# Gated attention and channel MLP on one core: q and k stored by SyncE, ten shared x/y tiles, and another order of the attention

## The chip, the cores and the metric

The kernel runs on one core of a Trainium2 chip. A core has five engines that run side by side and meet at semaphores: TensorE (PE in the profile) multiplies matrices into the accumulator memory PSUM, VectorE (DVE), ScalarE (ACT) and GpSimd (POOL) work elementwise, and SyncE (SP) issues transfers; ScalarE issues some too. The metric is the device time of one execution in microseconds, as the median of several runs.

## The reference, cut to what matters

The input x has 2048 tokens of 512 features. Two branches are computed from it and mixed per token.

```python
qkv = (x @ wqkv)                        # 32 heads of 16 features
scores = q k^T / 4, masked to 0 <= i - j < 256
a = softmax(scores) v, heads joined, @ wo
y = layernorm(x)                        # no scale, no shift
b = gelu(y @ w1 + b1) @ w2 + b2         # 512 -> 1792 -> 512
g = sigmoid(sum(x * gate_w))
out = g * a + (1 - g) * b
```

## The kernel before

Every matmul of the projections and of the MLP is made of three: each operand is split into a rounded high part and the remainder (high x high, high x low, low x high). The work has three stages.

**Stage one: projections.** Tokens come in four chunks of 512. Loads of x go into space of the value tile `vs`, and are split into tiles of the tag `x8` (eight buffers, L174). A table of letters, `UNITS` (L53), gives the order of 46 units of twelve matmuls: "a" and "q" are `qk_unit`s (L287) of the first and of the other three head groups, "v" are `v_unit`s (L311). Other work hangs on unit numbers through `at(n, ...)` and, some units later, through `after(k, ...)`: the loads of x (`FETCH`), the clearing of value space (`ONES`), loads of the weights (`WQS`), of the stacked q and k for the attention (`STACKS`), the statistics of the layer norm (`stat_unit`), and the normalized y (`load_y`, L469). A unit of q or k ends in `qk_out` (L297): ScalarE copies the high part out of PSUM, VectorE subtracts the low part, and both are stored to device memory. Here ScalarE issues the stores of the high part (L303), SyncE those of the low part (L304). `load_y` loads a tile of x transposed, subtracts the mean and multiplies by the inverse deviation on GpSimd (L484, L485), and splits it into `x8` tiles. The first ten of the first head quad's sixteen S are done in this stage too (L562).

**Stage two: attention and the first MLP layer.** The string `ORDER` (L38) gives the order, letter by letter. "S" (`s_pair`, L334) computes scores of one block of 128 queries for two heads, and VectorE masks them and takes the maximum (L352, L353). The maxima go through device memory into rows of q. "T" (`st_pair`, L378) computes the scores transposed, ScalarE takes the exponential into a tile `p` (L389), and GpSimd masks it (L391). "P" (`pv`, L399) multiplies two blocks of p by the values and their row of ones (L406). "f" is one step, two matmuls, of a first-layer unit of 24 steps (`mlp1_unit`, L586, L598), whose result goes to device memory as `hp`. S, T, P and a whole unit of f take their PSUM from a ring of four pairs of banks: S, T and P the one that was used longest ago, a unit of f holds one for its 24 steps.

**Stage three: the second MLP layer and the output projection.** 56 steps `mlp2(c, f)` of twelve matmuls (L809) add up to four accumulators per chunk. Before step (c, f), a tile of `hp` is loaded, ScalarE applies gelu (L657), and VectorE splits it (L661, L124). `attn_out(c)` (L757) loads the sums of the exponentials, inverts them (L765), scales the attention and multiplies by wo (L788). The last operation (L814) adds both branches, and SyncE stores the result (L815).

Of the kernel before, what the change touches and what calls it, by code (L numbers as in the profile page):

```python
# [60 lines left out]
def gated_mix_kernel(ctx, tc: tile.TileContext, xt, x2, wqk, wv, wo, xa, gw, w1, w2, b1, b2, out):  # L61
# [25 lines left out]
    def t2(dt=F32, shape=(128, 512)):  # L87
        return get("work", "t", nt[0], shape, dt)
# [41 lines left out]
    todo = {}  # L130

# [36 lines left out]
    nt[0] = 15  # L168
# [5 lines left out]
    def x8():  # L174
        return get("x", "x8", 8, (128, 2048), F32R)
# [45 lines left out]
    def load_x(c):  # L221
# [665 lines left out]
```

## Time and profile before

| what | value |
|---|---|
| median of three runs | 723.28 us (720.11 to 723.95) |
| the profiled execution's own time | 723.94 us |
| its span on the core | 722.2 us |
| mean granted clock of TensorE | 0.995 |
| stage one ends, attention starts | 150.0 us |
| last P ends | 515.7 us |
| last matmul ends | 716.4 us |
| busy share of TensorE, VectorE, ScalarE, GpSimd | 97%, 68%, 51%, 37% |
| matmuls | 5738 |

A row of the timeline has the start, the time, the engine, the line of the program, the operation, what it writes and reads, and in brackets the idle time of the engine before it and what ended that. "PEld" is TensorE's loading of weights, which overlaps its matmuls; "SPq" and "ACTq" are the engines' issuing of transfers. Ends of matmuls are modelled, so the distance between the starts of two matmuls says how fast they follow each other. A row of busy time by stretches has the stretch, its length, the busy time of PE, PEld, DVE, ACT and POOL, TensorE's granted clock, the busy share of the DMA engines, and GB/s. In a group of instructions, busy time and mean nanoseconds stand behind the bar.

### The profile page before, as it was taken

The numbers are of one execution on the slowest core, as the hardware profiler recorded it, in microseconds if no ns is written. First come the engines' busy times: TensorE is split into PE (matmuls) and PEld (weight loads), VectorE is DVE, ScalarE is ACT, GpSimd is POOL, SyncE is SP. The second block draws the span as 40 slices with busy tenths as digits, with TensorE's granted clock in tenths as the row PEclk, the third lists the DMA queues.
The fourth block names the chain that finished last, engine by engine and source line by source line (L and its number), as shares of the span: only waits on it lengthen the run. The fifth ranks groups of instructions, "written<-read, shape, count | busy, mean of one in ns | idle before, by whom it ended". The sixth has DMA issues, their size and how long they took to land.

```text
span 722.2 us, 16129 instructions
## 1 busy us (share of the span) xinstructions
PE 701.7 (97%) x5738; PEld 544.8 (75%) x5738; DVE 492.3 (68%) x1050; ACT 370.1 (51%) x584; POOL 264.3 (37%) x544
## 2 busy tenths in 40 slices
PE   8989999989999999999999999999899999999997
PEld 6867777866778777787777777776677788888886
DVE  5338986878886877868777787776364835735654
ACT  5332223457675666676766767667542413324131
POOL 8210007949665555554655547546200000000000
PEclk9999999999999999999999999999999999999999
DMA  8899958876577765476754654635574544443531
GB/s 270 259 276 306 302 170 272 259 214 206 176 217 225 247 199 168 128 229 216 216 186 157 189 170 134 195 108 172 183 260 155 176 131 154 145 134 109 185 113 58
DMA packets 104675, 138.46 MB, mean 192 GB/s; under 512 B 15668, under 2 KB 55540, under 8 KB 104468
## 3 DMA queue, kind: packets, MB, share of 16 engines
q1 hardware_dynamic: 97828, 125.63, 55.6%
q10 hardware_dynamic: 6768, 11.80, 4.9%
q8 instruction: 46, 0.75, 0.4%
q14 instruction: 33, 0.27, 0.1%
HBM read 82.06 MB, written 54.28 MB: 189 GB/s over the span
## 4 chain that ended last, share of the span: by engine, by line
PE 80%; DMA 7%; DVE 5%; SPq 3%; POOL 2%; issue 1%; ACT 1%; DVEq 0%; ACTq 0%; POOLq 0%
PE ps_b L598 20%; PE ps_a L809 16%; PE ps_d L293 11%; PE ps_b L406 10%; PE ps_b L387 7%; PE ps_b L343 6%; PE ps_o L788 5%; PE ps_d L318 4%; DVE mx L353 2%; DMA t<-in_wqk 2%; DMA qk<-t 1%; POOL p L391 1%; DVE ps_b L352 1%; SPq L772 1%; SPq L773 1%
## 5 line engine op out<-in xcount | busy, mean ns | idle before, releaser
L391 POOL TENSOR_SCALAR_AFFINE_SELECT p<-p 128x256 f32<-128x256 f32 x480 | 184.2, 413 | 137.1 <-ACT p L389 133.9
L598 PE MATMUL ps_b<-x,w 64*128 64x512 f32 x1344 | 223.5, 396 | 0.5 <-DVE mx L353 0.4
L389 ACT ACTIVATE p<-ps_b 128x768 f32<-128x768 f32 (+2 forms) x256 | 191.4, 772 | 55.0 <-PE ps_b L387 48.2
L809 PE MATMUL ps_a<-x,t 128*128 128x512 f32 x648 | 150.7, 390 | 1.6 <-DVE t L661 1.6
L353 DVE TENSOR_REDUCE mx<-ps_b 128x2 f32<-128x512 f32 x208 | 144.1, 693 | 7.2
L809 PEld LDWEIGHTS ps_a<-x,t 128*128 128x128 f32 x648 | 121.3, 188 | 28.2 <-issue 1.8
L598 PEld LDWEIGHTS ps_b<-x,w 64*128 64x128 f32 x1344 | 134.1, 187 | 8.0 <-PE ps_b L343 0.7
L352 DVE COPY_PREDICATED ps_b<-tri,ps_b 128x256 f32<-128x256 uint8 x208 | 88.4, 425 | 48.2 <-PE ps_b L343 43.5
L387 PE MATMUL ps_b<-q,k 64*128 64x384 f32 (+5 forms) x512 | 97.5, 365 | 3.5 <-DVE mx L353 2.4
L406 PE MATMUL ps_b<-p,v 128*32 128x128 f32 (+1 forms) x1920 | 91.5, 329 | 1.1 <-DVE mx L353 0.7
L343 PE MATMUL ps_b<-k,q 62*128 62x384 f32 (+3 forms) x472 | 87.4, 350 | 2.9 <-DVE mx L353 1.3
L406 PEld LDWEIGHTS ps_b<-p,v 128*32 128x32 f32 x1920 | 54.4, 110 | 36.7 <-issue 5.2
L127 ACT ACTIVATE t<-ps_b 128x256 f32<-128x256 f32 (+1 forms) x114 | 52.7, 489 | 56.4 <-PE ps_b L406 44.2
L387 PEld LDWEIGHTS ps_b<-q,k 64*128 64x128 f32 (+1 forms) x512 | 52.6, 185 | 32.0 <-PE ps_b L343 15.6
L343 PEld LDWEIGHTS ps_b<-k,q 62*128 62x128 f32 x472 | 48.8, 185 | 19.7 <-PE ps_b L387 5.8
L124 DVE TENSOR_TENSOR t<-t,t 128x512 fp32r<-128x512 f32 x70 | 48.5, 692 | 14.8 <-ACT t L127 11.9
L127 ACT ACTIVATE t<-t 128x512 fp32r<-128x512 f32 x16 | 10.1, 632 | 82.9 <-DVE t L776 36.9
L657 ACT ACTIVATE t<-t,b1s 128x512 f32<-128x512 f32 x56 | 38.0, 715 | 23.6 <-DMA t<-hp 23.1
L788 PE MATMUL ps_o<-wo,t 128*128 128x512 f32 x192 | 46.6, 392 | 0.8 <-ACT t L127 0.8
L318 PE MATMUL ps_d<-wv,x 128*128 128x512 f32 x192 | 46.0, 392 | 0.0
L293 PE MATMUL ps_d<-x,w 128*128 128x512 f32 x192 | 45.6, 392 | 0.0
L127 ACT ACTIVATE t<-ps_d 128x512 fp32r<-128x512 f32 x32 | 19.1, 596 | 51.3 <-PE ps_d L293 40.8
(79 smaller groups left out, 607.1 us busy)
## 6 DMA issues: line engine op xcount, KB each, us to landing
t<-hp SPq DMA_DIRECT2D x56, 256.0 KB
hp<-t SPq DMA_DIRECT2D x54, 256.0 KB
k<-qk SPq DMA_DIRECT2D x112, 98.0 KB
q<-qk SPq DMA_DIRECT2D x112, 98.0 KB
qk<-t ACTq DMA_DIRECT2D x40, 256.0 KB
qk<-t SPq DMA_DIRECT2D x32, 256.0 KB
osc<-t SPq DMA_DIRECT2D x31, 256.0 KB
t<-in_w SPq DMA_DIRECT2D x28, 256.0 KB
```

The lines of the kernel that those rows point to most:

```text
L127: act.activation(dst, src, AF.Copy)
L293: pe.matmul(o, a[:, dt * 128:(dt + 1) * 128], b[:, dt * C:(dt + 1) * C], start=n == 0, stop=n == 11)
L343: pe.matmul(o[:, e, :n], qs[pr][r:k, qb * 128:qb * 128 + 128], ks[pr][r:k, t0:t0 + n], start=True, stop=True)
L352: dve.copy_predicated(o[:, :, :128], tri, o[:, :, 256:384])
L353: dve.tensor_reduce(m, o[:, :, :256], mybir.AxisListType.X, ALU.max)
L387: pe.matmul(o[:, e, :w], ks[pr][r:k, kb * 128:kb * 128 + 128], qs[pr][r:k, kb * 128:kb * 128 + w], start=True, stop=True)
L389: act.activation(pt[:, :, :w], o[:, :, :w], AF.Exp, scale=0.25)
L391: pool.affine_select(out=pt[:, :, a:a + 128], in_=pt[:, :, a:a + 128], pattern=[[0, 2], [sgn, 128]], base=b, channel_multiplier=-sgn, comp ...
L406: pe.matmul(a[32 * h:32 * h + 32, at:at + w], vs[:, kb, v:v + 32], pts[p, kb][:, h, fr:fr + w], start=n == 0, stop=n == len(parts) - 1, sk ...
L598: pe.matmul(o[:, e], w[kt // 4][r:r + 64, k, m:m + 128], y[r:r + 64, a:a + C], start=n == 0, stop=n == 23)
L788: pe.matmul(a, x[:, g], wos[g][:, k], start=n == 0, stop=n == 11)
L809: pe.matmul(accs[c][b], x[:, b * 128:(b + 1) * 128], w, start=f == 0 and n == 0, stop=f == FT - 1 and n == 2)
```

## The change

Line numbers shift; the parts are these.

- Stores of q and k. All of them, high and low, are issued by SyncE one unit later, as one piece `send`; ScalarE issues none.
- Stage one's numbers. `UNITS` keeps the same kinds and counts of units in another order behind the sixteenth. The loads of x chunks two and three come at units 0 and 7 instead of 3 and 8, and their splits at 7 and 10; the other tables move too. The general ring `t` has 14 buffers instead of 15.
- Ten x/y tiles. The last chunk of x has two tiles of its own, `xq`. All sixteen tiles of y are then loaded and normalized in stage one (before, the last four came at the start of the attention); `YD` puts the last four of them on VectorE. In the attention `xq` serves as two of the eight tiles of p, and `t` has nine buffers instead of eleven.
- `ORDER` is another string with the same numbers of letters, and there is no empty P at its start.
- The load of the gelu table, the first two gelus and their splits are issued with the last T (`first_h`), ahead of the last f and the last three P.
- Layer two. Its eight accumulators take the four pairs of banks in the order in which these were last used (`pairs`, `tags`). The first tiles loaded there have a tag of their own, "e", and their gelus come before the split of two weight tiles. The sums of the exponentials are loaded at the third step of chunk zero instead of the fifth, and their inversion comes four steps later instead of two. The last block's sum and store are made in halves, the second stored by ScalarE.
- Assertions (`done`) are added; they issue nothing.

```diff
-ORDER = ("STPSTTSTSfTfTffSfTffSffSPTSffTfSffTfSfffSfTfTffffSPTSTSSTPTSTfffSffTTfffSPSfTfSfffTfTffSfSffffTPTfSf"
+ORDER = ("STTSTSfffTSffTfTffTSffTffTfSPSffTSfffTfSffTfSffSPTSTPSTfSffSfTSfffTfSfSfPTSffTffSfTffTffTSffTffSfSPS"
...
-UNITS = "vvaavvvaavvvaavq" + 7 * "qqqv" + "qq"
-FETCH = ((3, 2, 8), (8, 3, 13))
-ONES = 2, 6, 11, 14
-STACKS = 4, 8, 13, 18
-WQS = 9, 10, 14, 15, 16, 17
+UNITS = 'vvaavvvaavvvaaqvqqvqqqqvqqvqqqvqqvqqqqqvqvqqqq'
+FETCH = ((0, 2, 7), (7, 3, 10))
+ONES = (2, 7, 10, 14)
+STACKS = (5, 13, 17, 25)
+YS = (27, 35)
+STAT = (7, 26)
+SPS = (13, 16, 19, 22, 25, 28, 31, 34, 37, 41)
+YD = (12, 13, 14, 15)
+W1S = (42, 55)
+WQS = (7, 7, 12, 8, 13, 14)
...
-    nt[0] = 15
+    nt[0] = 14
...
-        h, l = x8(), x8()
+        h, l = (x8() if c < 3 else x8("xq", 2) for _ in range(2))
...
-        for k in (0, 1 + t)[:1 + (g == 0)]:
-            act.dma_start(f32(view(d, [S, DH], [50 * S, HG], [1, C], off=k * DH * S + c * C)), f32(h))
-        after(1, lambda: sp.dma_start(f32(view(d, [S, DH], [50 * S, HG], [1, C], off=(2 - t) * DH * S + c * C)), f32(l)))
+
+        def send():
+            for k, src in ((0, h), (1 + t, h), (2 - t, l)):
+                if src is l or k == 0 or g == 0:
+                    sp.dma_start(f32(view(d, [S, DH], [50 * S, HG], [1, C], off=k * DH * S + c * C)), f32(src))
+            done.add(("qk", g, t, c))
+
+        after(1, send)
...
-            pts[p, kb] = get("work", "p", 8, (128, 4, 384))
+            n = (NB * p + kb) % 8
+            if n % 4 == 3:
+                pts[p, kb] = x8("xq", 2, F32)[:, :1536].rearrange("p (h q) -> p h q", h=4)
+            else:
+                pts[p, kb] = get("work", "p", 6, (128, 4, 384))
...
+            eng = dve if 8 * cp + s in YD else pool
...
-    at(30, lambda: load_y(0, 0, KT, 3, pool))
-    at(37, lambda: load_y(1, 0, KT // 2, 3, pool))
+    at(YS[0], lambda: load_y(0, 0, KT, 3))
+    at(YS[1], lambda: load_y(1, 0, KT, 3))
...
-    after(1, lambda: load_y(1, KT // 2, KT, 2, pool, 4))
...
                 st_pair(p, kb, pr)
+                if not lt:
+                    first_h()
...
+    def first_h():
+        t = spare[0]
+        for f, (gelu, parts) in enumerate(early):
+            gelu()
+            parts((t[:, f * 2 * C:f * 2 * C + C], t[:, f * 2 * C + C:f * 2 * C + 2 * C]))
...
-    nt[0] = 44
+    nt[0] = -6
...
-    low, high = {"o0": 1, "o1": 1, "a4": 1, "a5": 1}, {f"a{i}": 1 for i in range(4)}
-    open_psum(*((low, high) if "b0" in used else (high, low)))
+    pairs = dict(zip(ring, (("a0", "a1"), ("a2", "a3"), ("a4", "a5"), ("o0", "o1"))))
+    tags = [tag for key in sorted(pairs) for tag in pairs[key]]
+    open_psum({tag: 1 for tag in tags})
...
-        after(2, inv)
+        after(4, inv)
         for b in range(4):
-            after(3 + b, lambda b=b: loads(b))
+            after(5 + b, lambda b=b: loads(b))
...
-                dve.scalar_tensor_tensor(out=u, in0=accs[c][b], scalar=g1[:, i:i + 1], in1=u, op0=ALU.mult, op1=ALU.add)
-                sp.dma_start(out[i], u)
+                for n in range(1 + (i == NB - 1)):
+                    k = slice(n * 256, n * 256 + 256) if i == NB - 1 else slice(0, D)
+                    dve.scalar_tensor_tensor(out=u[:, k], in0=accs[c][b][:, k], scalar=g1[:, i:i + 1], in1=u[:, k],
+                                             op0=ALU.mult, op1=ALU.add)
+                    (act if n else sp).dma_start(out[i, :, k], u[:, k])
...
-        if f == (4 if c == 0 else 2):
+        if f == 2:
             attn_out(c)
```

What the numbers and the string do is seen in the order of the instructions. The first place is SyncE's queue in stage one, at the fourth chunk of x: `v` is the value tile that the raw x is loaded into, `k` and `q` the stacks that are read back from the stored `qk`, `t` a general tile. Before:

```order
L227 DMA v_84<-in_xt 128x512 x4
L330 DMA k_5_82<-qk_1_66 98x512
L330 DMA q_3_80<-qk_0_65 98x512
L330 DMA k_6_83<-qk_1_66 98x512
L330 DMA q_4_81<-qk_0_65 98x512
L212 DMA t_386<-in_wqk 128x512
L304 DMA qk_0_65<-t_402 16x8x512
L212 DMA t_409<-in_wqk 128x512
```

Now, at the same chunk:

```order
L320 DMA qk_1_66<-t_317 16x8x512 x2
L320 DMA qk_1_66<-t_318 16x8x512
L238 DMA v_84<-in_xt 128x512 x4
L454 DMA gws_104<-in_gw 128x512
L455 DMA b1s<-in_b 128x14
L459 DMA t_355<-in_xa 128x512
L218 DMA t_358<-in_wqk 128x512
L218 DMA t_361<-in_wqk 128x512
```

The two weight loads stand behind the load of x with no reading of stacks between them; the stores of the high parts (two with the first group) have come into this queue.

The second place is TensorE in the middle of the attention. `ps_b` is a pair of banks of the ring; "k,q" in L343 is an S, "q,k" in L387 a T, "x,w" in L598 is f, and "p,v" in L406 is P. Before:

```order
L343 MATMUL ps_b_664_3988<-k_6_83,q_4_81 128x384 x2
L598 MATMUL ps_b_668_3999<-x_221_1247,w_3348 128x512 x2
L387 MATMUL ps_b_670_4013<-q_3_80,k_5_82 128x384 x2
L598 MATMUL ps_b_668_3999<-x_221_1247,w_3348 128x512 x2
L387 MATMUL ps_b_671_4021<-q_4_81,k_6_83 128x384 x2
L598 MATMUL ps_b_668_3999<-x_221_1247,w_3348 128x512 x4
L598 MATMUL ps_b_668_3999<-x_272_1537,w_3349 128x512 x4
L343 MATMUL ps_b_672_4035<-k_5_82,q_3_80 128x384 x2
```

Now (L369 is S, L417 T, L633 f):

```order
L369 MATMUL ps_b_682_4098<-k_5_82,q_3_80 128x384 x2
L417 MATMUL ps_b_683_4103<-q_4_81,k_6_83 128x384 x2
L633 MATMUL ps_b_667_3996<-x_233_1311,w_3333 128x512 x6
L369 MATMUL ps_b_684_4115<-k_6_83,q_4_81 128x384 x2
L633 MATMUL ps_b_667_3996<-x_233_1311,w_3333 128x512 x2
L633 MATMUL ps_b_667_3996<-x_214_1200,w_3332 128x512 x4
L417 MATMUL ps_b_686_4132<-q_3_80,k_5_82 128x384 x2
L369 MATMUL ps_b_687_4138<-k_5_82,q_3_80 128x384 x2
```

S and T come more often side by side, with longer runs of f between them. Neighbours of S and T in the whole string are 55 before and 124 now; a P follows a P four times before and nine times now.

The third place is ScalarE at the end of the attention. L389 are the last exponentials, L127 reads PSUM (`ps_b`) to a general tile, L657 is the gelu. Before:

```order
L389 ACTIVATE p_7715<-ps_b_1264_7716 128x2x128
L389 ACTIVATE p_7715<-ps_b_1265_7725 128x2x128
L127 ACTIVATE t_7760<-ps_b_1259_7688 128x512
L616 DMA hp<-t_7760 128x512
L127 ACTIVATE t_7763<-ps_b_1259_7688 128x512
L616 DMA hp<-t_7763 128x512
L657 ACT_TABLE_LOAD
L657 ACTIVATE t_7640<-t_7640,b1s 128x512
```

Now:

```order
L419 ACTIVATE xq_7722<-ps_b_1261_7723 128x2x128
L419 ACTIVATE xq_7722<-ps_b_1262_7728 128x2x128
L692 ACT_TABLE_LOAD
L692 ACTIVATE t_7653<-t_7653,b1s 128x512
L692 ACTIVATE t_7655<-t_7655,b1s 128x512
L132 ACTIVATE t_7741<-ps_b_1244_7611 128x512
L651 DMA hp<-t_7741 128x512
L132 ACTIVATE t_7744<-ps_b_1244_7611 128x512
```

The table load and the gelus have moved ahead of the copies of the last f; the copies of the last P stand behind these.

More of the change, by code (lines that the diff above doesn't have):

```diff
@@ L130, in gated_mix_kernel @@
     todo = {}
+    done = set()
     def after(k, fn):
@@ L212, in load_w, with rest @@
         sp.dma_start(raw, wqk[g, t])
-        return lambda: split(w, raw)
+        def rest():
+            split(w, raw)
+            done.add(("wq", g, t))
+        return rest
     def load_wv(dt):
@@ L241, in rest @@
                 lo(dt)
+            done.add(("x", c))
         return rest, hi, lo
@@ L283, in first_units @@
             fn()
+        done.update([("x", 0), ("wv", 0)])
         for t in range(2):
@@ L287, in qk_unit @@
     def qk_unit(g, t, c):
+        assert (g == 0 or ("wq", g, t) in done) and ("x", c) in done
         o = ps("d")
@@ L309, in double, with ones @@
             sp.dma_start(to, fr)
+    def ones(c):
+        assert ("x", c) in done
+        pool.memset(vs[:, 4 * c:4 * c + 4], 1.0)
+        done.add(("v", c))
     def v_unit(b):
         c, i = divmod(b, 4)
+        assert {("v", c), ("wv", 0)} <= done
         o = ps("d")
@@ L325, in load_stacks @@
         g, j = divmod(p, 2)
+        assert {("qk", g, t, a // C) for t in range(2)} <= done
         held_cols[p] = a + n
@@ L330, in load_stacks @@
                 sp.dma_start(f32(dst[14:112, a:a + n]), f32(src))
-    mxs, done = {}, set()
+    mxs = {}
     def s_pair(p, qb, pr):
@@ L436, in rest @@
                                      accum_out=z[:, i:i + 1])
+            done.add(("st", i))
         after(3, rest)
     def stat_end():
+        assert {("st", i) for i in range(NB)} <= done
+        done.add("stat")
         ve = small("ve", 1, (128, NB))
@@ L692, in gated_mix_kernel @@
     ls = [(p, qb, pr) for p in range(8) for qb in range(NB) for pr in range(2)][2 * (NB - LAG):]
-    lp = [None] + [(p, j) for p in range(8) for j in range(NB // 2)]
+    lp = [(p, j) for p in range(8) for j in range(NB // 2)]
     def run(order):
@@ L707, in run @@
                 if a:
[L708 removed]
+                    pv(*a, lt and not ls)
             else:
                 fill()
+    def first_h():
[3 more added lines that the diff above has]
+            parts((t[:, f * 2 * C:f * 2 * C + C], t[:, f * 2 * C + C:f * 2 * C + 2 * C]))
     run(ORDER)
     flush()
[L714 to L727 removed]
+    run("P")
     settle()
@@ L739, in gated_mix_kernel @@
         waiting[0, f] = load_h(0, f)
-    for f in range(4, 6):
-        waiting.pop(("w", f))()
-    while jobs or cur[0]:
-        fill()
+    nt[0] = 38
     flush()
```

71 lines of the change are left out of this document (31 added, 40 removed).

## The prediction

> **What bounds the kernel now.** I read the page's first part and then the busy time by stretches. TensorE sets the end.
>
> ```profile
> span 722.2 us, 16129 instructions
> PE 701.7 (97%) x5738; PEld 544.8 (75%) x5738; DVE 492.3 (68%) x1050; ACT 370.1 (51%) x584; POOL 264.3 (37%) x544
> ...
> 56.03:150.01 93.98, 93.98 (x421) 74.06 (x420) 78.75 (x171) 29.49 (x52) 34.57 (x24) 1.00 0.80 254
> 150.01:190.00 39.99, 35.06 (x383) 25.49 (x384) 32.00 (x73) 27.00 (x41) 29.63 (x57) 0.96 0.66 202
> 190.00:470.00 280.00, 278.27 (x3294) 211.82 (x3296) 215.08 (x509) 194.01 (x300) 154.11 (x380) 1.00 0.62 192
> 470.00:515.68 45.68, 44.37 (x581) 32.06 (x572) 27.04 (x57) 30.96 (x50) 25.18 (x64) 1.00 0.42 132
> ```
>
> The columns are the stretch, its length, and the busy time of TensorE, its weight loads, VectorE, ScalarE and GpSimd. The change adds and removes no matmul, so what it can win is time in which TensorE stands idle or runs slowly. Idle are 4.93 us at the start of the attention (39.99 - 35.06), 1.73 in its 280 us of steady state and 1.31 at its end; layer two's start has 2.07 and 1.36 more (rows below). The rest hides before 56.03. The chain of waits and the timeline show it; 12 projection matmuls take 2.72 us there (5.44 for 24); the last of these three rows is used further down.
>
> ```profile
> 12.34 5.44 PE ps_d L318 x24
> 39.15 7.88 DMA t<-in_wqk
> ...
> 509.47 3.47 PE ps_b L598 x30
> ...
> 35.16 0.34 SPq L330 DMA_DIRECT2D k<-qk  x1
> 39.15 0.36 SPq L212 DMA_DIRECT2D t<-in_wqk  x1
> 47.05 0.63 ACT L127 ACTIVATE w<-t 128x512 fp32r<-128x512 f32 x1 [1.45 <-DMA t<-in_wqk]
> 47.59 2.17 ACT L127 ACTIVATE x<-v 128x512 fp32r<-128x512 f32 x4
> 48.26 7.84 PE L293 MATMUL ps_d<-x,wx 128*128 128x512 f32 x24 [2.12 <-ACT x L127]
> ```
>
> SyncE issues the second weight load of group one at 39.15, behind its waits for the stacks; it lands 7.88 us later. ScalarE waits for it with the fourth chunk of x queued behind, and TensorE waits 2.12 us for that chunk. The next matmuls run to 56.03, 7.77 us for 24 instead of 5.44. Short windows say why.
>
> ```profile
> 45.63:49.05 3.42, 1.28 (x5) 0.46 (x3) 1.54 (x4) 2.00 (x4) 0.00 (x0) 1.00 0.96 273
> 49.05:52.46 3.41, 3.41 (x8) 2.44 (x8) 3.38 (x14) 1.21 (x3) 1.59 (x1) 0.50 0.72 209
> 151.45:154.86 3.41, 2.23 (x16) 1.29 (x18) 3.31 (x7) 2.99 (x4) 2.25 (x6) 1.00 0.99 267
> ```
>
> After a window with 1.28 us busy the granted clock is 0.50 for 3.41 us, some 1.7 us lost. The window from 151.45, busy for 2.23, is followed by another such drop: the 0.96 granted over the 39.99 us from 150.01 is 3.4 us at half.
>
> **Change by part, against the profiled run's own 723.94 us** (1.74 around the span; 0.66 above the median of the three runs).
>
> *Stage one.* SyncE now issues x's fourth chunk and both weight loads before the second chunk's stacks, and the two splits stand at unit 10 instead of 12 and 13. SyncE reaches them behind the first stacks and six more stores; in the trace the second stacks leave at 35.16, so I let the weights leave by then and land 7.88 us later, at 43, before the 46.1 (48.26 - 2.12) at which TensorE ran dry. Stall and half clock are 2.12 + 2.33 = 4.45; bounds 0 and 4.5, I take **-4.2**. The 40 stores of q and k that leave ScalarE add an issue each to SyncE's queue; behind them stand stack and y loads that have three units of 2.72 us in hand, so I price them at nothing (their loss is a rival below).
>
> A rule weighed: the Trainium skill, "TensorE: Matmul & The Clock Gate", Part 1, has the clock halve after an idle window of about 3.4 us. The windows above were busy for 1.28 and 2.23 us and still cost it, so the rows differ. By the page the stall is worth its 2.12 alone, and the sum below would end 2.1 higher.
>
> *Start of the attention.* GpSimd still normalizes four y tiles there, between the masks that P waits for:
>
> ```profile
> 161.89 1.29 POOL L484 TENSOR_TENSOR t<-t,t 128x512 f32<-128x512 f32 x1 [4.13 <-DMA t<-in_x]
> 164.50 3.37 POOL L391 TENSOR_SCALAR_AFFINE_SELECT p<-p 128x256 f32<-128x256 f32 x8
> ...
> L353 DVE TENSOR_REDUCE mx<-ps_b 128x2 f32<-128x512 f32 x208 | 144.1, 693 | 7.2
> L389 ACT ACTIVATE p<-ps_b 128x768 f32<-128x768 f32 (+2 forms) x256 | 191.4, 772 | 55.0 <-PE ps_b L387 48.2
> ```
>
> Now all sixteen tiles are done in stage one, the last four on VectorE: GpSimd loses four tiles of 2.6 us (161.89 to 164.50), 10.4 in all, in this stretch. VectorE gains eight subtractions and multiplications and the four splits, some 8 us at about 0.69 in the last seven units (19 us); the first score blocks then wait about 1 us longer for it. At stake are the 4.93 idle less a steady 0.25, and 1.7 of clock: 6.4 at best, and a loss of 2 if VectorE is late. I take **-3.0**, near the middle, since the first 8 us (scores waiting for VectorE) stay.
>
> *Another order.* Here TensorE runs a unit's step of two matmuls (f, L598) in 0.23 us (3.47 for fifteen), a score block for maxima (S, L343) or for the exponential (T, L387) in 0.18, and P (L406) in 1.44:
>
> ```profile
> 268.18 0.34 PE L343 MATMUL ps_b<-k,q 48*128 48x384 f32 x2
> 268.45 1.51 PE L406 MATMUL ps_b<-p,v 128*32 128x256 f32 x32
> 269.89 0.44 PE L343 MATMUL ps_b<-k,q 62*128 62x384 f32 x2
> 270.17 0.34 PE L387 MATMUL ps_b<-q,k 64*128 64x384 f32 x2
> 270.35 0.40 PE L598 MATMUL ps_b<-x,w 64*128 64x512 f32 x2
> ...
> 350.57 0.44 PE L343 MATMUL ps_b<-k,q 62*128 62x384 f32 x2
> 350.82 0.37 PE L387 MATMUL ps_b<-q,k 64*128 64x384 f32 x2
> ...
> 474.17 0.33 PE L387 MATMUL ps_b<-q,k 64*128 64x128 f32 x2 [0.46 <-DVE mx L353]
> ...
> PEld ps_b L406 <- ACT p L389: 4.8, 17, 0.4
> PEld ps_b L406 <- POOL p L391: 2.6, 8, 0.6
> ```
>
> First, P's distance. With these durations the work between a block's last T and the P that reads it has a median of 3.5 us before and 5.7 now; shorter than 1.6 (0.77 for the exponential, two masks of 0.42, the eighth of 3.37) are twelve P before and none now. The two waits say 7.4 us on the weight loads; TensorE's own share is smaller, since a matmul still runs. Bounds 0 and 7.4, I take **-2.5**. Second, edges. An S takes 0.27 before a P and 0.28 after it, 0.1 more than alone; nine P follow a P instead of four, each saving about 0.23: **-1.2**. Third, neighbours. S and T stand side by side 124 times instead of 55. At 270.17 a T took 0.18 before an f; at 350.57 an S took 0.25 before a T. Between nothing and 0.075 for 69: 0 to 5.2, I take half, **+2.6**. At the end of the stage P no longer chases T: of the 1.31 idle, **-0.8** (bounds 0, 1.3).
>
> *Start of layer two, and the tail.*
>
> ```profile
> 514.07 0.60 ACT L127 ACTIVATE t<-ps_b 128x512 f32<-128x512 f32 x1 [0.50 <-ACT t L127]
> 514.70 0.33 ACTq L616 DMA_DIRECT2D hp<-t  x1
> 515.12 1.28 ACT L657 ACT_TABLE_LOAD   x1 [0.45 <-ACT t L127]
> 516.41 1.33 ACT L657 ACTIVATE t<-t,b1s 128x512 f32<-128x512 f32 x2
> 517.74 5.92 PE L809 MATMUL ps_a<-x,x 128*128 128x512 f32 x24 [2.07 <-DVE x L661]
> 536.64 0.95 DVE L765 RECIPROCAL su<-su 128x128 f32<-128x128 f32 x1 [3.39 <-DMA su<-osc]
> 538.62 8.64 PE L809 MATMUL ps_a<-x,t 128*128 128x512 f32 x36 [1.36 <-DVE t L661]
> 555.56 2.37 DMA t<-hp
> 716.42 2.79 DVE L814 SCALAR_TENSOR_TENSOR us<-ps_a,g,us 128x512 f32<-128x512 f32 x4 [2.38 <-PE ps_a L809]
> ```
>
> TensorE waits 2.07 us for table load, gelu and cast. In the change the load and both gelus follow the last exponential directly, while TensorE still has one f and three P, about 4.7 us. Late next is the PSUM: layer two's first accumulators take the bank of the last f. ScalarE frees it after two exponentials (about 1.0, an estimate from L389), 1.28, 1.33, two copies of 0.60 and an issue of 0.33: 5.1 us. The wait is then 0.4, a gain of 1.67. The third hidden tile comes next. Its load still needs the memory of the last P; behind it ScalarE now runs two gelus and two weight copies, VectorE two subtractions, and only then its cast: 0.35 + 2.37 + 1.4 + 1.3 + 0.69 + 0.43 = 6.5 us after the last P, against 0.4 + 5.44 of work in hand: +0.7. The sums' loads leave two steps (5.4 us) earlier while the reciprocal keeps its step, so its 3.39 us wait ends, and TensorE's 1.36 behind it. Together **-2.3** (bounds -3.6, +0.2).
>
> A rule weighed: the Trainium skill, "ScalarE: Activation LUTs", What ACT_TABLE_LOAD costs, adds a drain of 1.38 us to the 1.28 of a load. Here the load starts 0.09 after the issue ahead of it ended (514.70 + 0.33) and the gelu right at its end, so the rows show no such drain. By the page the accumulators would come 1.4 later and the sum would be 1.4 higher.
>
> The last block's sum and store go out in halves on two queues: about half of one 0.75 us operation and of a transfer, **-0.4** (0 to -0.8).
>
> Sum: -4.2 - 3.0 - 2.5 - 1.2 + 2.6 - 0.8 - 2.3 - 0.4 = -11.8. 723.94 - 11.8 = 712.1, 711.5 against the median.
>
> **Rivals.** *The attention gains more (0.12):* both P waits go wholly (another -4.9), the start gives its 6.4 (-3.4) and neighbours cost nothing (-2.6): about 701. For it: twelve short distances become none. Against: the score blocks, which wait for VectorE too, are as many as before.
>
> *SyncE becomes late (0.13).* It issues 40 more stores, each behind its unit's VectorE split, and the weight loads stand behind them. For it: 7.88 us of landing there, with 0.72 to 0.99 of the DMA engines' time taken (last column but one of the windows). Then the stall stays (+4.2) and one more of its size comes, 4.4: about 720. The Trainium skill, "DMA: Bandwidth & Descriptors", Issuing engines are not separate DMA queues, says that all issuers share the same DMA engines and a second one saves issue time alone; by that the move brings no bandwidth. No run here shows it yet.
>
> *Neighbours wait for banks (0.09), the slower side.* S and T share three free banks beside f's. Side by side, a T can find its bank under VectorE's mask and maximum, as at 474.17, where 0.46 us stood idle. If two in three of the 69 new neighbours pay that, it is 21 us in place of 2.6: 730. From 31 of them on (14.3 us), the whole gain is gone. Against: clusters are followed by longer runs of f, and the work between two uses of a bank, counted as for P, keeps its median of about 1.5 us.
>
> *The change does part of what it says (0.06):* the start and layer two give nothing: 717.
>
> **How the numbers follow.** The forecast has 0.60 and its own range is 705 to 718. A measurement tells 0.5% from no change: faster is below 719.7, slower above 726.9. Forecast, larger gain and partial gain are faster (0.78), and half of SyncE's case is too, less what the forecast's upper edge loses: 0.80. Same 0.12, slower 0.08. The range reaches from the larger gain to SyncE's case: 701 to 721.
>
> **What would show it.** No idle over 1 us of TensorE between 40 and 56 us and no clock of 0.50 there; no y tile on GpSimd after 150 us; both P waits near zero; layer two's first matmul idle under 1 us, with ScalarE's copy as releaser, and the third tile late by under 1.5; no reciprocal wait. Wrong would be: new idle of S and T behind the maxima, or SyncE's queue late for weights or y.

## The result and the profile after

The changed kernel takes 705.03 us (702.76 to 707.69, median of four runs), the kernel before in the same session 723.28 (median of three; a fourth execution, of 1351 us, is left out as slow). The ratio is 0.975, with a 95% interval from 0.972 to 0.979: faster, by 18.3 us. The prediction said 711.5, in a range from 701 to 721. Measured again in a later session, the changed kernel took 704.94 (701.23 to 706.51, six runs) against 724.19: ratio 0.973 (0.970 to 0.976). The profiled execution took 704.66, so between the two profiled executions 19.3 us have gone, where the sum of the prediction had 11.8.

The first part of the page of the changed kernel, and then its busy time by stretches: the start of the attention, 263 us of its steady state, its last 45.7 us, and layer two with the tail.

```profile
span 702.9 us, 16160 instructions
PE 686.8 (98%) x5738; PEld 547.1 (78%) x5738; DVE 487.5 (69%) x1057; ACT 368.9 (52%) x586; POOL 253.6 (36%) x536
...
145.56:185.55 39.99, 37.90 (x406) 28.86 (x407) 34.29 (x82) 28.16 (x42) 21.75 (x58) 0.96 0.61 183
185.55:449.04 263.49, 260.16 (x3230) 207.50 (x3227) 206.78 (x491) 188.11 (x293) 149.54 (x367) 1.00 0.65 200
449.04:494.72 45.68, 45.68 (x620) 36.43 (x616) 32.07 (x67) 33.55 (x53) 26.89 (x68) 1.00 0.46 145
494.72:702.90 208.18, 199.55 (x865) 161.16 (x864) 112.53 (x192) 65.35 (x104) 0.00 (x0) 1.00 0.47 151
```

The matmuls are the same 5738, and TensorE is busy for 14.9 us less: part of what is gone was never shown as idle, it lay inside rows of matmuls that followed each other late. By stages, with the boundaries of the kernel before (150.0, 515.7, 722.2): stage one ends 4.45 earlier, the attention is 349.2 us instead of 365.7 (16.5 less, where the prediction had 4.9), and layer two with the tail 208.2 instead of 206.5 (1.7 more, where the prediction had 2.7 less).

Stage one, in the timeline of TensorE around the place of the old stall:

```profile
43.21 3.00 PE L343 MATMUL ps_d<-wv,x 128*128 128x512 f32 x12
46.04 5.60 PE L307 MATMUL ps_d<-xq,wx 128*128 128x512 f32 x24
```

No idle time stands in brackets, and the 24 matmuls on the fourth chunk take their 5.6 us. The weight loads leave at 34.34, not late, as priced.

For the attention one needs stretches with the same work. Both orders have issued the same 43 S, 43 T, 10 P and 98 f before their 195th place, and the same 167 S, 168 T, 41 P and 478 f between the 195th and the 1049th. Between these two points the kernel before took:

```profile
214.46:456.36 241.90, 240.63 (x2861) 183.97 (x2859) 182.36 (x443) 167.72 (x259) 132.42 (x327) 1.00 0.61 189
```

and the changed one:

```profile
204.81:440.32 235.51, 232.32 (x2861) 186.62 (x2860) 184.91 (x446) 167.81 (x260) 133.31 (x328) 1.00 0.64 196
```

6.4 us less in steady state. From the start of the first score block to the first point it is 59.3 instead of 64.5, from the second point to layer two's first matmul 55.0 instead of 61.4, of which 1.5 belong to layer two. The waits between the same two points say where. The rows hold the engine, the tile and line, whom it waited for, the sum in us, how often, and the longest. Before:

```profile
PEld ps_b L387 <- PE ps_b L343: 9.3, 34, 0.6
PEld ps_b L343 <- PE ps_b L387: 4.0, 14, 0.6
PEld ps_b L406 <- ACT p L389: 3.3, 11, 0.3
PEld ps_b L406 <- POOL p L391: 1.0, 4, 0.3
```

and after (L417 is T, L369 S, L436 P):

```profile
PEld ps_b L436 <- ACT p L419: 2.7, 10, 0.3
PE ps_b L417 <- DVE ms L389: 2.1, 1, 2.1
PEld ps_b L436 <- ACT xq L419: 1.6, 5, 0.3
PEld ps_b L417 <- PE ps_b L369: 0.7, 3, 0.3
```

The wait of T's weights behind an S falls from 9.3 to 0.7, and that of S behind a T, 4.0 before, is not listed any more. P's waits for exponential and mask, which the prediction hoped to end, are still there: 4.3 before, 5.0 now (2.7 and 1.6, and 0.7 in two short waits for the mask). New is a single wait of T for its maxima of 2.1, at 241 us; another of 1.0 follows at 331. Without these two the changed kernel's 235.5 would be 232.3.

What is the wait of T behind S? The profile names TensorE itself as the releaser. A place in the kernel before shows more (rows of TensorE and VectorE, some left out):

```profile
256.85 0.38 PE L343 MATMUL ps_b<-k,q 62*128 62x384 f32 x2
257.15 0.86 PE L406 MATMUL ps_b<-p,v 128*32 128x256 f32 x16
257.53 0.42 DVE L352 COPY_PREDICATED ps_b<-tri,ps_b 128x256 f32<-128x256 uint8 x1
257.94 0.44 PE L343 MATMUL ps_b<-k,q 62*128 62x384 f32 x2
257.99 0.69 DVE L353 TENSOR_REDUCE mx<-ps_b 128x2 f32<-128x512 f32 x1
258.22 0.49 PE L598 MATMUL ps_b<-x,w 64*128 64x512 f32 x2
258.79 0.21 PEld L387 LDWEIGHTS ps_b<-q,k 64*128 64x128 f32 x2 [0.39 <-PE ps_b L343]
258.82 0.45 PE L387 MATMUL ps_b<-q,k 64*128 64x384 f32 x2
```

S, T and P take the three free banks of the ring in turn. The T at 258.82 is the third use after the S at 256.85, so it takes that S's bank. VectorE's mask and maximum on that bank end at 257.99 + 0.69 = 258.68; T starts 0.14 later. The unit step f ahead of it, 0.23 us, began at 258.22: TensorE had nothing since 258.45, though the row of f, whose end is modelled, hides most of it. In the changed kernel, such a bank has one f more of time (the rows of f and others are left out):

```profile
297.74 0.34 PE L369 MATMUL ps_b<-k,q 62*128 62x384 f32 x2
298.45 0.38 PE L417 MATMUL ps_b<-q,k 64*128 64x384 f32 x2
298.65 0.69 DVE L379 TENSOR_REDUCE mx<-ps_b 128x2 f32<-128x512 f32 x1
299.09 0.37 PE L417 MATMUL ps_b<-q,k 64*128 64x384 f32 x2
299.73 0.27 PE L369 MATMUL ps_b<-k,q 62*128 62x128 f32 x2
```

The S at 299.73 takes the bank of the S at 297.74; VectorE ended at 299.34, 0.39 earlier, and nothing waits. Summed with the prediction's durations, the time from an S to the next S or T on its bank has a median of 1.52 us in the old order and 1.75 in the new, one f more; under 1.6 us are 124 of 216 before and 53 of 217 now. 1.6 is about what VectorE needs: from the start of an S to the end of its maximum the traces have a median of 1.64 us, so 1.46 after the 0.18 that the sum counts for the S, and then the 0.14. The traces show the waiting itself when each use of a bank is followed around the ring: between 185 and 460 us, 79 of 166 uses that follow an S began within 0.16 us of the end of VectorE's maximum on that bank in the kernel before, and 15 of 171 in the changed one.

Layer two, in some rows of TensorE's and SyncE's timelines, and the last rows of TensorE and VectorE, which set the end:

```profile
495.30 5.78 PE L841 MATMUL ps_a<-x,x 128*128 128x512 f32 x24 [0.58 <-ACT t L132]
501.24 22.35 PE L841 MATMUL ps_a<-x,t 128*128 128x512 f32 x96 [0.16 <-DVE t L696]
514.95 0.61 SPq L804 DMA_DIRECT2D t<-osc  x1
518.02 0.61 SPq L805 DMA_DIRECT2D t<-rd  x1
525.64 3.01 PE L820 MATMUL ps_o<-wo,t 128*128 128x512 f32 x12 [2.06 <-ACT t L132]
...
692.75 2.88 PE L820 MATMUL ps_o<-wo,t 128*128 128x512 f32 x12
695.47 2.88 PE L841 MATMUL ps_a<-x,t 128*128 128x512 f32 x12
696.39 0.75 DVE L823 SCALAR_TENSOR_TENSOR us<-b2s,g,us 128x512 f32<-128x512 f32 x1 [3.56 <-ACT us L822]
697.06 2.85 DVE L848 SCALAR_TENSOR_TENSOR us<-ps_a,g,us 128x512 f32<-128x512 f32 x5
```

The first matmul waits 0.58 instead of 2.07, with ScalarE's copy as its releaser, and the reciprocal's 1.36 behind VectorE is gone. New is the 2.06 at the first output matmul: SyncE stands before the first load of the reciprocals (518.02) until they have been stored, some 2.5 us, with the loads behind it. The size of this wait isn't fixed: with the same code of layer two it is 0.91 us in the run with the old order below, 1.04 in a second profiled execution of the changed kernel, and 3.05 in the run with neighbours pulled apart. And in every later chunk the output matmuls now come two steps later, next to the chunk's end. In the last chunk the kernel before had its last output matmuls at 707.38, ahead of 36 matmuls of layer two; now twelve of these are left, and VectorE adds the bias (L823) just when the four final sums could begin.

### The profile page after: what moved, and what is told of

It is laid out like the page before. It is cut to its first block, busy times and chain, and to the rows that moved or that the text cites. A ratio compares the mean times of both kernels' runs of the same rounds, so it can differ in the third digit from the quotient of the medians.

```text
span 702.9 us, 16160 instructions
## 1 busy us (share of the span) xinstructions
PE 686.8 (98%) x5738; PEld 547.1 (78%) x5738; DVE 487.5 (69%) x1057; ACT 368.9 (52%) x586; POOL 253.6 (36%) x536
## 4 chain that ended last, share of the span: by engine, by line
PE 87%; DVE 4%; DMA 4%; SPq 3%; ACT 1%; issue 1%; ACTq 0%; DVEq 0%
PE ps_b L633 22%; PE ps_a L841 15%; PE ps_d L307 12%; PE ps_b L436 11%; PE ps_b L417 7%; PE ps_b L369 6%; PE ps_d L343 6%; PE ps_o L820 5%; DVE us L848 1%; SPq L805 1%; SPq L804 1%; PE ps_d L292 1%; PE ps_x L369 1%; DMA osc<-t 1%; DMA t<-in_wqk 1%
## 5 line engine op out<-in xcount | busy, mean ns | idle before, releaser
L633 PE MATMUL ps_b<-x,w 64*128 64x512 f32 x1344 | 212.8, 394 | 0.0
L421 POOL TENSOR_SCALAR_AFFINE_SELECT p<-p 128x256 f32<-128x256 f32 x368 | 140.8, 412 | 124.2 <-ACT p L419 122.5
L419 ACT ACTIVATE p<-ps_b 128x768 f32<-128x768 f32 x192 | 148.0, 796 | 41.7 <-PE ps_b L417 35.5
L633 PEld LDWEIGHTS ps_b<-x,w 64*128 64x128 f32 x1344 | 134.2, 187 | 6.6 <-PE ps_b L417 0.3
L417 PE MATMUL ps_b<-q,k 64*128 64x384 f32 (+5 forms) x512 | 92.9, 348 | 4.5 <-DVE ms L389 2.1
L369 PE MATMUL ps_b<-k,q 62*128 62x384 f32 (+2 forms) x472 | 87.1, 345 | 0.8 <-DVE t L129 0.7
L436 PE MATMUL ps_b<-p,v 128*32 128x256 f32 (+1 forms) x1472 | 72.4, 330 | 0.1
L417 PEld LDWEIGHTS ps_b<-q,k 64*128 64x128 f32 (+1 forms) x512 | 52.4, 185 | 23.3 <-issue 10.0
L436 PEld LDWEIGHTS ps_b<-p,v 128*32 128x32 f32 x1472 | 42.1, 110 | 23.6 <-ACT p L419 2.4
L369 PEld LDWEIGHTS ps_b<-k,q 62*128 62x128 f32 (+1 forms) x472 | 48.9, 186 | 12.0 <-issue 4.8
L421 POOL TENSOR_SCALAR_AFFINE_SELECT xq<-xq 128x256 f32<-128x256 f32 x112 | 43.4, 413 | 35.2 <-ACT xq L419 34.9
L129 DVE TENSOR_TENSOR t<-t,t 128x512 fp32r<-128x512 f32 x66 | 45.7, 692 | 14.4 <-ACT t L132 11.9
L419 ACT ACTIVATE xq<-ps_b 128x768 f32<-128x768 f32 (+1 forms) x64 | 44.3, 706 | 16.5 <-PE ps_b L417 13.3
```

Source lines behind the costliest of these rows:

```text
L369: pe.matmul(o[:, e, :n], qs[pr][r:k, qb * 128:qb * 128 + 128], ks[pr][r:k, t0:t0 + n], start=True, stop=True)
L417: pe.matmul(o[:, e, :w], ks[pr][r:k, kb * 128:kb * 128 + 128], qs[pr][r:k, kb * 128:kb * 128 + w], start=True, stop=True)
L419: act.activation(pt[:, :, :w], o[:, :, :w], AF.Exp, scale=0.25)
L421: pool.affine_select(out=pt[:, :, a:a + 128], in_=pt[:, :, a:a + 128], pattern=[[0, 2], [sgn, 128]], base=b, channel_multiplier=-sgn, comp ...
L436: pe.matmul(a[32 * h:32 * h + 32, at:at + w], vs[:, kb, v:v + 32], pts[p, kb][:, h, fr:fr + w], start=n == 0, stop=n == len(parts) - 1, sk ...
L633: pe.matmul(o[:, e], w[kt // 4][r:r + 64, k, m:m + 128], y[r:r + 64, a:a + C], start=n == 0, stop=n == 23)
```

## The experiments

All kernels are the changed kernel with the edit named; the times are medians, beside 704.9 to 705.0 for the changed kernel. They were taken in three sessions, in which the kernel before took 723.05, 723.72 and 724.19 us. The interval of a ratio to it is 1 to 3 us wide to either side, so differences of less than about 3 us between two runs aren't clear.

**The old order alone.** ORDER is the old string, with its idle first P:

```
-    lp = [(p, j) for p in range(8) for j in range(NB // 2)]
+    lp = [None] + [(p, j) for p in range(8) for j in range(NB // 2)]
```

> The changed kernel with the old order string alone (new loads in stage one, new y tiles, new start of layer two are kept). Theory 1, the order: the attention went from 365.7 to 349.2 us, 16.5 less, and some 4 of that lie at its start, where the y tiles moved. So the old order gives back about 12: 717 us (715 to 719). Rival, the order matters little and the attention gained from the y tiles, the moved loads and the memory of p: 705 to 709.

716.36 us (716.12 to 717.23). The order is worth 11.4 us of the 18.3. Between the two points:

```profile
208.42:450.55 242.13, 240.88 (x2860) 184.29 (x2858) 182.28 (x443) 167.64 (x259) 132.43 (x327) 1.00 0.61 188
```

and among the waits:

```profile
PEld ps_b L417 <- PE ps_b L369: 9.1, 33, 0.6
```

The 241.9 us and the 9.3 of wait of the kernel before are back, though the loads, y tiles and gelus are the new ones.

**The old order without VectorE's mask.** The line that holds the bank for 0.46 us is left out, so the maxima are taken over two unmasked blocks of three:

```
-            dve.copy_predicated(o[:, :, :128], tri, o[:, :, 256:384])
```

> The run before (old order) with VectorE's mask ahead of the maximum left out (the maxima are then taken over two unmasked blocks of three; P, exp and the sums are computed as ever). A score block's bank comes free 0.46 us earlier. Theory 1a, banks: in the old order a bank that held a score block S is wanted again 1.52 us after it (steps summed), in the new one 1.75, and VectorE gives it back 1.26 to 1.6 us after it; waits for that and the f behind them are some 9 us of the kernel before. Without the mask the old order loses them: 9 less than the run with the mask, about 708. Theory 1b, P: the twelve short distances between exp and P are what the old order costs; VectorE's mask has no part in them: within 2 of the run with the mask, 715 to 717.

708.78 us (707.96 to 709.31), 7.6 less than with the mask. Between the two points:

```profile
209.98:442.62 232.64, 231.86 (x2860) 181.85 (x2856) 128.89 (x301) 166.72 (x259) 131.94 (x327) 1.00 0.64 197
```

9.5 us less, for the 9 that theory 1a expected, and no row of T's weights waiting behind an S is left. VectorE's hold on the bank was the cause, under the name of another engine; that it isn't simply VectorE's load is seen in the next run. (In all it is 7.6 by the medians. In the profiled executions the start of the attention is 1.5 slower, its end 2.2 quicker, and layer two, whose code is the same, 3.0 slower: its first output matmul waited 3.21 us there and then ran at half clock.)

**The new order without the mask.** The same line left out of the changed kernel.

> The changed kernel, its own order, with the same mask left out. Theory 1a (banks): the new order already gives the bank its time, so little is left: 1 to 3 less than the changed kernel, 702 to 704, most of it at the start of the attention. If the mask costs the new order as much as the old one (8 or more), 1a is wrong: VectorE is then simply a bound of both.

708.57 us (707.87 to 709.68): 3.6 more, not 1 to 3 less. Between the two points it is 236.3, against 235.5 with the mask: no gain to be seen there any more. If VectorE's load were the bound, the new order would have gained some 9 as well. A gain of 1 to 2, as theory 1a has it, may hide in the 236.3, since 3.8 us of single waits near 242 and 249 and one stretch of half clock (some 1.7) lie in it, against 3.2 of single waits in the changed kernel. The loss is at the start of the attention, where ScalarE's third exponential waits in both kernels without the mask:

```profile
154.47 1.51 ACT L418 ACTIVATE p<-ps_b 128x768 f32<-128x768 f32 x2 [6.61 <-DMA qk<-t]
```

Its tile lies on memory that the last stores of q and k still read, and SyncE issued these at 149.2 and 150.0; TensorE stood for 5.85 us and then ran for 10 us at half clock. The changed kernel issues its last two stores at 149.22 and 150.10, without that wait. Why the mask's absence brings it is open.

**Long distances of P in the old order.** Thirteen P moved later by a few places.

> The changed kernel with the old order again, in which only the thirteen P that follow their block's last T within 2 us (steps summed) are moved later, past a few f, S and T, so that all have over 2 us. The short times of a score block's bank stay (124 under 1.6 us in the old order, 125 here). Between the same two points of the program (167 S, 168 T, 41 P and 478 f) the kernel before took 241.9 us, the changed one 235.5, the old order in the changed kernel 242.1. Theory 1a, banks: 241 to 243 there, 715.5 to 717 in all. Theory 1b, P's distance, priced at 2.5 us by the prediction and 7.4 at most: 2.5 to 7 less than the old order: 709 to 714.

725.02 us (724.21 to 728.83), 8.7 more than the old order; between the points 247.8 against 242.1. Theory 1b finds no support: P had over 2 us of distance everywhere, and its waits for exponential and mask between the points only went from 3.8 to 3.3 us. They hardly depend on the distance. Theory 1a's 242 was too low as well. A moved P shifts the banks of all between its old and its new place: some 40 S banks, instead of some 30, were then wanted within 1.4 us, and units f waited for their bank too. An estimate from the distances between starts of matmuls, less the usual time of a step: behind banks still held after an S, TensorE lost about 10 us between the points, and about 6 in the old order. So this run shows no gain from distance, but does not measure it alone.

**Neighbours pulled apart in the new order.** `STff` becomes `SfTf`, 72 times; of the 124 neighbours that the prediction counted, 108 are an S beside a T, and 41 of these stay.

> The changed kernel's own order with 72 of its neighbours S T or T S pulled apart by the f that follows them (108 neighbours become 41); P keeps its places. Score blocks whose bank is wanted again within 1.6 us go from 53 to 76. The prediction priced neighbours at 0.0375 us each: 2.5 less, 702.5. Theory 1a: neighbours cost nothing, and 23 more short bank times at about 0.1 to 0.15 each cost 2 to 3: 706 to 708, and 237 to 238 between the two points named with the run before.

710.26 us (707.02 to 711.47), 5.3 more. Between the points:

```profile
206.31:443.64 237.33, 234.93 (x2861) 186.21 (x2860) 185.01 (x447) 167.97 (x260) 132.91 (x328) 1.00 0.64 195
```

and among the waits:

```profile
PEld ps_b L417 <- PE ps_b L369: 2.8, 11, 0.3
```

1.8 us slower there, and the wait of T behind S goes from 0.7 to 2.8, as the short bank times go from 53 to 76. Pulling neighbours apart costs; and that neighbours cost nothing is seen in the changed kernel's own trace, where between 185 and 450 us the next matmul starts 0.18 us after an S (median) before a T as before an f, and 0.18 after a T before either. The rest of the difference between the profiled executions is spread: 0.5 in stage one, 1.0 at the start and 1.0 at the end of the attention, 0.6 in layer two. Other executions of the new order repeat its end to 0.1, so that 1.0 belongs to the edit too; the rest is within what executions differ by.

**The last four y tiles as before**, on GpSimd in the attention.

```
-YD = (12, 13, 14, 15)
+YD = ()
...
-    at(YS[1], lambda: load_y(1, 0, KT, 3))
+    at(YS[1], lambda: load_y(1, 0, KT // 2, 3))
...
+    after(1, lambda: load_y(1, KT // 2, KT, 2, 4))
```

> The changed kernel with the last four y tiles loaded and normalized as before: in the attention, on GpSimd. The prediction's step for the start of the attention: 3.0 more, 708 (up to 711), in the first 60 us after 145. Rival: VectorE, which now has these tiles in its last units, is what the first score blocks wait for (0.75 at 147.1, 1.32 at 148.9 in the changed kernel); without them the start is quicker and the end of the stage pays nothing: 703 to 705.

711.24 us (709.08 to 712.52), 6.3 more. From just ahead of the first score block to the first point, in this run and then in the changed kernel:

```profile
145.48:209.26 63.78, 58.94 (x657) 43.48 (x658) 51.49 (x113) 42.60 (x67) 43.30 (x88) 0.97 0.67 207
```

```profile
145.44:204.81 59.37, 57.14 (x657) 43.15 (x658) 49.82 (x112) 41.28 (x64) 31.93 (x80) 0.97 0.65 198
```

4.4 us, with 11.4 us more of work on GpSimd: the step was right, and somewhat small at 3.0. The rest of the 6.3 isn't from this step's place: 1.2 lie between the two points, where a wait and a stretch of half clock fell.

**The old places of the loads in stage one.**

```
-FETCH = ((0, 2, 7), (7, 3, 10))
+FETCH = ((3, 2, 8), (8, 3, 13))
-ONES = (2, 7, 10, 14)
-STACKS = (5, 13, 17, 25)
+ONES = (2, 7, 11, 14)
+STACKS = (5, 8, 13, 18)
...
-WQS = (7, 7, 12, 8, 13, 14)
+WQS = (9, 10, 14, 15, 16, 17)
```

The order of the units stays the new one, and the first stacks come at unit 5 instead of the old 4.

> The changed kernel with the old places of the loads of x's fourth chunk, of the weights of q and k and of the stacks in stage one. The prediction's step: TensorE's stall near 46 us and the half clock behind it come back, 4.4 more in stage one, 709.5 in all. Rival: part of the stall came from ScalarE's stores of q and k, which this run leaves with SyncE: 1 to 2 more, 706 to 707.

711.63 us (709.55 to 712.70), 6.7 more. The stall is back, and with it the half clock, here for two windows of 3.41 us; the timeline of TensorE and then two stretches of busy time:

```profile
48.95 8.52 PE L307 MATMUL ps_d<-xq,wx 128*128 128x512 f32 x24 [3.26 <-ACT xq L132]
```

```profile
47.73:51.14 3.41, 2.19 (x5) 1.39 (x6) 3.38 (x9) 3.21 (x6) 0.00 (x0) 0.50 0.61 213
51.14:54.56 3.42, 3.42 (x10) 2.65 (x9) 2.64 (x13) 0.00 (x0) 1.96 (x1) 0.50 0.76 178
```

Stage one's last matmul ends at 151.5 instead of 145.6. The expectation was 4.4; the stall is longer here (3.26 for 2.12) and the clock stays low for twice the time.

**ScalarE's stores of q and k.** The high parts go out from ScalarE again.

> The changed kernel with the stores of the high parts of q and k issued by ScalarE again. The prediction priced the move at nothing: within 1.5 us of the changed kernel. Rival A: SyncE is late with them (its last two stores leave at 149.2 and 150.1, behind 1 MB of weights): 2 to 4 less. Rival B: ScalarE's 0.6 us issues were what made its copies late in stage one: 2 or more slower.

707.20 us (704.87 to 713.44) beside 704.94 in the same session; the ratios to the kernel before, 0.977 (0.974 to 0.980) and 0.973 (0.970 to 0.976), just overlap. It leans to rival B: in the profiled execution, its slowest, stage one ends 1.6 later than in the changed kernel beside it, and T waits 2.15 us for VectorE's low part. The price of nothing may have been 2 us off; it isn't settled.

**The reciprocal one step earlier in layer two.**

```
-        after(4, inv)
+        after(3, inv)
```

> The changed kernel with the reciprocal and its store one step (2.7 us) earlier in layer two's attention output, the loads that read it unmoved. Theory 2: layer two's 2.06 us wait of the first output matmul is SyncE standing 2.5 us before the first of these loads until the reciprocals have landed; one step earlier they have: 2.0 to 2.7 less (0.34 and 0.39 behind it go too), about 702.7. Rival: the sums' loads land too late for the earlier reciprocal, VectorE waits there instead and the hidden tile behind it too: same or slower, 705 to 707.

707.23 us (704.25 to 707.67): 2.3 more, which isn't clear of noise, and not the 2.0 to 2.7 less. The rival came: the wait moved.

```profile
517.02 0.95 DVE L797 RECIPROCAL su<-su 128x128 f32<-128x128 f32 x1 [4.78 <-DMA su<-osc]
...
518.99 11.50 PE L841 MATMUL ps_a<-x,t 128*128 128x512 f32 x48 [1.73 <-DVE t L696]
```

VectorE stands 4.78 us at the sums, which were issued 6.3 us before, and the hidden tile behind it is late by 1.73. The output matmul's 2.06 is gone; layer two is 201.5 from its first to its last matmul instead of 203.1. In the profiled execution the attention, whose code is unchanged, took 4.0 more than in the changed kernel's, which is more than the step won.

**The changed kernel again, and two attempts at more**, in one session. The first attempt moves the copies of q and k for two groups to a quieter time, six loads of maxima one block earlier, and layer two's sums and reciprocal both one step earlier; the second also pulls the first thirteen f forward:

```
-ORDER = ("STTSTSfffTSffTfTffTSffTffTfSP...
+ORDER = ("SffTfTfSTfSfTSfTfTffTSfTffTSP...
```

> The changed kernel itself, beside the three runs that follow, on one chip. 703 to 707. Theory 3: what differs between its executions are single waits of 1 to 3 us, at the start of the attention (145 to 152) and where T waits for its maxima near 240, since there the DMA engines are busy for 0.7 to 1.0 of the time.

> The changed kernel with three repairs: (1) the copies of q and k for groups two and three leave in the third and fifth pair of heads' turn instead of the second and fourth, where the transfers share is 0.4 to 0.6; (2) six loads of maxima leave one block earlier; (3) layer two's loads of the sums and the reciprocal with its store leave one step earlier, the loads that read it unmoved. Theory: (1) and (2) take the wait of T near 241 (2.15 us) and 331 (about 1.3), (3) the 2.06 at the first output matmul: 3.5 to 5.5 less than the changed kernel run beside it, 699.5 to 702. Rival: the copies meet another transfer where they now are, and SyncE stands at the early maxima until they are stored: 1 less or same.

> The run before, and the first 29 places of the order with the thirteen unit steps f pulled forward between the first S and T (S, T and P keep their own order), so that TensorE has work that needs nothing of VectorE while VectorE ends its last units. Theory: the idle 0.75 and 1.32 us at 147 to 149 go, and the half clock for 3.4 us behind them (1.7 us of work): 2 to 3.5 less than the run before. Rival: the first f need the weights and y tiles that land last, or the later T stand closer and wait for their banks: same to 2 slower.

704.94 (701.23 to 706.51), 704.10 (700.92 to 705.46) and 703.64 us (703.09 to 704.18); ratios to the kernel before 0.973, 0.971 and 0.972, each about 0.0025 wide to either side. Neither attempt can be told from the changed kernel, so the 3.5 to 5.5 and the 2 to 3.5 expected did not come. In the first, T's idle wait for its maxima, 1.81 us at 240 in the changed kernel beside it, is gone (0.15 of an S for VectorE is left there), but T waits 1.29 at 373, behind the turn to which the copies were moved; the first output matmul's wait falls from 1.04 to 0.74 and the third's rises to 0.92. In the second, the idle times at the start are 0.23, 1.07 and 0.52 instead of 0.74 and 1.31, hardly less in sum, and the clock was halved for 6.8 us behind them.

## Why the prediction was right, and where it was off

The way and stage one's mechanism were right. The time came out at the lower edge of the forecast's own 705 to 718, and that it came so near is partly luck: between the profiled executions the attention gained 11.6 us more than the sum had for it, mostly by a mechanism that the sum didn't price, and layer two did 4.4 worse, which hid part of that.

- **Stage one, -4.2:** measured -4.45 between the profiles; the old loads cost 5.8 there. Right. The weight loads left at 34.34, as assumed. The 40 stores moved to SyncE "at nothing" delayed nothing that is seen; ScalarE perhaps gains 2.
- **Start of the attention, -3.0:** 4.4 in the run that undoes it. Right in kind, small in size, and its clock half was no sure gain (below).
- **Another order, -1.9 in all:** the one large miss. The old order costs 11.4. "P's distance, -2.5" failed: P's waits for exponential and mask went from 4.3 us between the points to 5.0, though all distances are long now, and long distances in the old order won nothing. "Neighbours, +2.6" failed: a step takes the same 0.18 us beside a neighbour as beside an f, and pulling them apart made the kernel 5.3 slower. "Edges, -1.2" was not tested alone; a P right behind a P starts 1.32 us after it, any other step 1.44. What took their place is a term that the prediction had only as the rival of the slower side, with the sign turned: banks held by VectorE. It counted "the work between two uses of a bank" over all uses and found the same median of about 1.5 us in both orders. But a bank after an S is held until VectorE has done mask and maximum (1.64 us from the start of the S, median), one after a T until ScalarE's exponential ends (1.28). Times after an S went from 1.52 to 1.75, across the 1.6 that VectorE needs, while those after a T kept their median and lost a little on the mean. 9.5 us in steady state hung on it, shown by the run without the mask; the new order wins about that much and pays 3.2 in new waits for maxima. The row of that wait, 9.3 us between the two points, could be read before; its releaser's name, TensorE, hid the bank.
- **The end of the stage, -0.8:** 61.4 to 55.0 from the second point to layer two, less layer two's 1.5: -4.9; of these the old order gives back 3.8. Mis-sized for the same reason: only idle time was counted, and the bank waits lie inside busy rows.
- **Layer two's start and the tail, -2.7:** +1.7. The first wait is 1.5 shorter (1.67 priced), the reciprocal's gap is gone and the third tile is late by 0.16 (0.7 priced). The table load starts 0.02 us behind the last exponential and the first gelu 0.01 behind the load, so the sum was right to leave out a drain. What failed is "the sums' loads leave two steps earlier while the reciprocal keeps its step": that holds in the first chunk alone. There SyncE now waits for the store of the reciprocals, which cost the first output matmul 2.06 in this execution. In the others all comes two steps later: from the starts of the matmuls, the last two chunks are 0.72 and 0.74 us longer each, and from the last matmul's start to the end it is 4.95 us instead of 4.19. The halves of the last sum take 0.48 each, for 0.74 whole, so they could not bring the 0.4. Giving the later chunks their old steps back was not tried.

Of the rivals, "the attention gains more" came nearest (701 for a measured 705), though not through P's waits; "neighbours wait for banks" had the right mechanism with the wrong sign; SyncE was not late for the weights.

The parts undone one by one give 11.4 + 6.3 + 6.7 = 24.4, less layer two's loss 22.7, for 18.3 measured, so they aren't independent. Why is not shown; single waits and stretches of half clock, which come in one run and not in another, may be part of it.

## What to carry to other kernels

When an order of work is judged by the time between two uses of a buffer, count it by who holds the buffer, not over all uses, and hold it against that engine's measured time (here 1.64 us from the start of an S to the end of its maximum, and 0.14 until the next matmul on the bank). A wait that is named after the waiting engine itself, many times and a few tenths long, is worth a look for a bank behind it. And a step that is moved in a loop's first round moves in the others too: price those, and the tail.

## What the runs showed of the hardware

The same kernel with the same two waits (0.75 and 1.32 us, 0.74 and 1.31) at the start of the attention ran at half clock behind them in one execution and not in another. The first profiled execution, in stretches of 3.41 us:

```profile
145.21:148.62 3.41, 1.58 (x10) 0.66 (x8) 3.27 (x6) 2.52 (x4) 1.00 (x3) 1.00 0.74 208
148.62:152.03 3.41, 3.17 (x18) 2.95 (x20) 2.38 (x6) 1.34 (x2) 1.25 (x4) 0.50 0.98 240
```

and the second, 701.23 us:

```profile
143.53:146.95 3.42, 2.67 (x16) 1.78 (x14) 3.38 (x6) 1.76 (x4) 0.00 (x0) 1.00 0.59 170
146.95:150.36 3.41, 2.10 (x18) 1.59 (x20) 3.31 (x7) 2.06 (x4) 1.95 (x6) 1.00 1.03 279
```

All stretches of 0.50 within a run begin whole multiples of 3.41 us apart (49.05 and 154.86 in the kernel before: 31 of them; 47.73 and 160.38 in the run with the old loads: 33), so they lie on a grid, and where the grid cuts the two waits seems to decide: in one stretch they leave 1.58 us busy, in two 2.67 and 2.10. The Trainium skill, "TensorE: Matmul & The Clock Gate", Part 1, says that this window is free-running and does not reset with the kernel; the runs agree, since the grid lies at another distance from the start in the two executions above. It has an idle window as the condition, and here windows that were busy for 1.58 or, in the kernel before, 2.23 us were enough, while the 2.10 above was not, nor 1.60 in the run with the old loads (245.71 to 249.12); so the busy time of one stretch does not settle it, and what does is open. About 1.7 us of work hang on it each time, and the executions of the changed kernel differ by 5.

The second surprise is a wait for a small load among large ones: in all eight profiles of the new order with the copies in their old turns, TensorE stands idle near 240 us for 1.2 to 4.3 us in one or two waits of T or S, mostly for maxima on their way, while 0.6 to 0.9 of the DMA engines' time is taken in the changed kernel. The old order, with 4 us more (steps summed) between the load of these maxima and the T that needs them, shows no such wait, and the two kernels with the copies moved have 0.15 and 0.46 there, for VectorE. None of the six maxima loads that those two kernels issue earlier is the one that this T needs, so the copies were what held it up (whether in SyncE's queue or in the DMA engines isn't shown); in both, T waits for maxima further on (1.29 at 373, and 1.4 at 377 in the second).
